# Moving score products ahead of the weighted sums in the first rounds of an attention and mixture kernel

## The chip, the cores and the metric

The kernel runs on one core of a Trainium2 chip. The metric is the time of one execution in microseconds (us), as the median of several runs. A profile of one execution shows, engine by engine, when each instruction ran. The engines are TensorE (PE, with its weight loads shown apart as PEld), VectorE (DVE), ScalarE (ACT), GpSimd (POOL, which here mostly issues transfers) and SyncE (SP).

## The reference

The inputs are q, k and v of shape (4 batches, 8 heads, 768 positions, 64), a flag per head, and the weights of 8 experts. First comes attention with one of two masks per head:

```python
scores = scale * np.matmul(q, k.transpose(0, 1, 3, 2))
causal = rel >= 0
stream_keep = causal & (is_sink | in_win)      # 4 sink positions, window 64
mask = np.where(retr[0, :, 0, 0, None, None], full_mask, stream_mask)
a = softmax(np.where(mask, scores, -1e9))
x = (a @ v) reshaped to (3072, 512)
```

Then the 3072 rows of x go through a mixture: the gate's exponentials P are normalised eight times by rows and columns (Sinkhorn), and the result is

```python
for e in range(8):
    h = np.maximum(x @ w1[e], 0.0)
    out += P[:, e:e + 1] * (h @ w2[e])
```

## The kernel before, in words

The work of attention is cut into units (b, g, u): a batch, a group of 256 query positions (g = 0, 1, 2) and a half of the heads. A unit has two halves a, each for two heads. Every half takes its keys in g + 1 chunks of up to 512 columns; such a chunk is a task, and two tasks make a round. For the first batch, counting from zero as the code does, round 0 is unit g=0,u=0; round 1 is g=0,u=1; rounds 2 and 3 are the halves a=0 and a=1 of g=1,u=0; rounds 4 and 5 are those of g=1,u=1; with round 6 the group g=2 begins. The names in the profile leave the batch out or the unit out: `PT_1_0_1` is g=1, u=0, a=1, and `sc_1_0` is a=1, chunk 0.

A round goes through these steps.

- `emit_prep` (L230): 16 transposes on PE turn the loaded k and q of a unit into the tile `tr`, and DVE copies it out as `kT` (L243).
- `scores(n)` (L479, with the products at L424): PE multiplies keys by queries into two tiles `sc` in PSUM. There are two such tiles and no more, so the products of a round wait until ACT has read those of the round before.
- `soften` (L482): with index 0 it issues the exponentials on ACT (L433, tile `PT`), with index 1 the masks on DVE (L442, L445).
- `sum_later(n)` and `finish_sums` (L472, L459): PE sums v by the masked weights (L268) into the one tile `pv`; DVE takes a reciprocal and scales (L281, L282) into `xn`. As there is one `pv`, the next sum waits for that scaling.
- `turn` (L289): four transposes of `xn` on PE, then an ACT copy (L299) into `xT`, which is x transposed, the input of the mixture.
- `fill` (L453): pieces of the first expert's layers, put between rounds so that PE has work. A piece of layer 1 (L334) reads `xT` and ends with a DVE relu (L341); a piece of layer 2 (L348) reads the weights w2 (`w_0_133`) and ends with an ACT copy (L352). The pieces of layer 1 read both `xT_76` (heads of u=0) and `xT_77` (heads of u=1).
- `place_v(g)` (L110): the v of the first batch is loaded with pairs of positions in one partition (`vraw`, the tile `acc_84`). Four products with an identity matrix (L115) put a third of it in order, and two ACT copies (L119) write it into the tile `v_0`.
- `emit_vfar` (L248): DVE multiplies v by the mask of far keys (`farx`) into `vf` (L252). The sums over far keys read `vf` instead of v. `spell_far(2, ...)` (L207) is an ACT copy that makes the third slice of `farx`, which the `vf` of group 2 needs.

The products of PE, the transposes, the pieces of the first expert and others share the tag `mo`, three banks of PSUM used in turn; a tile waits for the reader of the tile three before it.

The rounds 0 to 5 are written out by hand from L490 to L541, under `manual_schedule` for PE, DVE and ACT: on these engines the instructions stand in the order in which the code writes them. Loads of k, q and v are issued on POOL, where the framework places them; each waits for the eighth load before it. From round 6 on (L542) a loop writes the rounds, and the framework's scheduler may place their instructions among the others; it had, for instance, put the `vf` of group 2 in among the work of round 4. After attention come the Sinkhorn steps (L564) and the remaining seven experts (from L599), which take most of the time.

Of the kernel before, what the change touches and what calls it, by code (L numbers as in the profile page):

```python
# [32 lines left out]
def kernel(  # L33
# [61 lines left out]
    def v_tile(b):  # L95
        if b not in vts:
            vts[b] = ap.tile([128, H, NC, DV], F16, tag="v16", name=f"v16_{b}")
            nc.vector.memset(vts[b][:, :, :, D:DV], 1.0)
        return vts[b]
# [10 lines left out]
    def place_v(g):  # L110
        for n in range(2):
            t = psA.tile([128, 512], F32, tag="mo", bufs=3, name=f"vp_{g}_{n}")
            rows = slice(64 * n, 64 * n + 64)
            for c in range(2):
                nc.tensor.matmul(  # L115
                    out=t[64 * c:64 * c + 64, :].rearrange("p (h d) -> p h d", h=H),
                    lhsT=ident16[rows, rows], rhs=vraw[g][rows, :, c, :], start=True, stop=True,
                )
            nc.scalar.activation(  # L119
                out=v_tile(0)[:, :, 2 * g + n, 0:D], in_=t.rearrange("p (h d) -> p h d", h=H),  # L120
                func=AF.Copy, bias=0.0, scale=1.0,
            )
# [73 lines left out]
    farx = cp.tile([128, H, 3, DV], F16, tag="farx")  # L196
# [10 lines left out]
    def spell_far(n, src):  # L207
        nc.scalar.activation(out=farx[:, :, n], in_=src, func=AF.Copy, bias=0.0, scale=1.0)
# [21 lines left out]
    def emit_prep(b, g, u):  # L230
        tr = psA.tile([128, 512], F32, tag="mo", bufs=3, name=f"tr_{b}_{g}_{u}").bitcast(F16)
        for i, src in enumerate(kq[b, g]):
            for a in range(2):
                for c in range(2):
                    for hh in range(2):
                        nc.tensor.transpose(
                            out=tr[64 * hh:64 * hh + 64, ts(4 * i + 2 * a + c, 128)],
                            in_=src[:, 4 * u + 2 * a + hh, c, :], identity=ident16,
                        )
        t = ap.tile([128, 2, 2, 256], F16, tag=f"kT{u}{g}", bufs=1 + (g == 0),  # L240
                    name=f"kT_{b}_{g}_{u}")
        kTs[b, g, u], qTs[b, g, u] = t[:, 0], t[:, 1]
        nc.vector.tensor_copy(  # L243
            out=t.rearrange("r i a (n c p) -> r (i a) c n p", c=2, p=64),
            in_=tr.rearrange("r (i c n p) -> r i c n p", i=4, c=2, p=64),
        )

    def emit_vfar(b, g):  # L248
        if b not in vfs:
            vfs[b] = ap.tile([128, H, 4, DV], F16, tag="vf", bufs=1, name=f"vf_{b}")  # L250
        n = 2 * g - 2
        nc.vector.tensor_tensor(out=vfs[b][:, :, n:n + 2, :], in0=vts[b][:, :, n:n + 2, :],  # L252
                                in1=farx[:, :, g - 1:g + 1, :], op=ALU.mult)
# [35 lines left out]
    def turn():  # L289
        while turns:  # L290
            b, g, u = turns.pop(0)
            xn = xns.pop((b, g, u))
            xt = psA.tile([128, 512], F32, tag="mo", bufs=3, name=f"xt_{b}_{g}_{u}").bitcast(F16)
            for a in range(2):
                for sb in range(2):
                    nc.tensor.transpose(out=xt[:, ts(2 * a + sb, 128)], in_=xn[:, a, sb],
                                        identity=ident16)
            c0 = b * S + 256 * g
            nc.scalar.activation(  # L299
                out=xT[u][:, :, c0:c0 + 256], in_=xt[:, 0:512].rearrange("p (a c) -> p a c", a=2),  # L300
                func=AF.Copy, bias=0.0, scale=1.0)
            if u == 1:
                one, two = first_steps(b, g)
                at = len(fillers) - 2 * ((b, g) == (0, 1))
                fillers[at:at] = one
                fillers.extend(two)
# [18 lines left out]
    def first_steps(b, g):  # L325
        w1, w2 = expw[0]
        c0 = b * S + 256 * g
        hT = [hp.tile([128, 512], F16, tag="hT", name=f"hT_0_{b}_{g}_{i}") for i in range(4)]

        def layer1(i):  # L330
            l1 = psA.tile([128, 512], F32, tag="mo", bufs=3, name="l1")
            for fb in (2 * i, 2 * i + 1):
                for dc in range(4):
                    nc.tensor.matmul(  # L334
                        out=l1[:, ts(fb % 2, 256)], lhsT=w1[:, dc, ts(fb, 128)],
                        rhs=xT[dc // 2][:, dc % 2, c0:c0 + 256], start=(dc == 0), stop=(dc == 3),
                    )
            if late[0]:
                nc.scalar.activation(out=hT[i], in_=l1, func=AF.Relu, bias=0.0, scale=1.0)
            else:  # L340
                nc.vector.tensor_scalar(out=hT[i], in0=l1, scalar1=0.0, scalar2=None, op0=ALU.max)  # L341
            return 1

        def layer2(sb):
            l2 = psA.tile([128, DM], F32, tag="mo", bufs=3, name="l2")
            for fc in range(8):
                o = 256 * (fc % 2) + 128 * sb
                nc.tensor.matmul(  # L348
                    out=l2, lhsT=hT[fc // 2][:, o:o + 128], rhs=w2[:, fc, :],
                    start=(fc == 0), stop=(fc == 7),  # L350
                )
            nc.scalar.activation(out=acc_of(b * NC + 2 * g + sb),  # L352
                                 in_=l2.rearrange("p (n d) -> p n d", n=2), func=AF.Copy,
                                 bias=0.0, scale=1.0)
            return 2

        return [partial(layer1, i) for i in range(4)], [partial(layer2, sb) for sb in range(2)]
# [3 lines left out]
    def run(g, n):  # L361
        for _ in range(n):
            if next(g, "end") == "end":
                return False
        return True
# [29 lines left out]
    PTs, sums, preps = {}, [], []  # L395
# [57 lines left out]
    def fill(n):  # L453
        while n > 0 and fillers:
            done = fillers.pop(0)()
            n -= done
            left[0] -= done

    def finish_sums(between=None):  # L459
        for i, ((gen, scale), key) in enumerate([(sums_of[key], key) for key in sums_of]):  # L460
            if i and between:
                between()
            while run(gen, 1):
                pass
            del sums_of[key]
            scale[0]()
# [5 lines left out]
    def sum_later(n):  # L472
        for i, a, ci in tasks[2 * n:2 * n + 2]:
            b, g, u = units[i]
            if ci == g:
                scale = []
                sums_of[i, a] = gen_pv(b, g, u, a, PTs.pop((i, a)), scale), scale

    def scores(n):  # L479
        return [emit_scores(*t) for t in tasks[2 * n:2 * n + 2]]  # L480

    def soften(pairs, which=(0, 1)):  # L482
        for pair in pairs:
            for w in which:
                pair[w]()

    def warm(n):
        keep_warm(ident16, kTs[units[0]].rearrange("p a s -> p (a s)"), n)

    engines = {mybir.EngineType.PE, mybir.EngineType.DVE, mybir.EngineType.Activation}  # L490
    with tc.manual_schedule(engines=engines):
        keep_warm(blank[:, 0:128], blank, 9)
        make_far()
        make_keep()
        round_first(0)
        emit_prep(*units[0])
        round_first(4)
        r0 = scores(0)
        soften(r0, (0,))
        make_masks((0, 1))  # L500
        emit_prep(*preps.pop())
        warm(3)
        r1 = scores(1)
        soften(r1[:1], (0,))
        place_v(0)
        soften(r0, (1,))
        sum_later(0)
        soften(r1[1:], (0,))
        make_masks((2, 3))
        emit_prep(*preps.pop())  # L510
        warm(2)
        r2 = []
        finish_sums(lambda: r2.extend(scores(2)))
        soften(r1, (1,))
        soften(r2, (0,))
        warm(2)
        turn()
        sum_later(1)
        emit_vfar(0, 1)
        finish_sums(lambda: emit_prep(*preps.pop()))  # L520
        place_v(1)
        soften(r2, (1,))
        sum_later(2)
        r3 = scores(3)
        soften(r3, (0,))
        turn()
        spell_far(2, farx[:, :, 1])
        finish_sums()
        soften(r3, (1,))
        sum_later(3)  # L530
        fill(1)
        soften(scores(4))
        finish_sums()
        sum_later(4)
        fill(1)
        emit_prep(*preps.pop())
        soften(scores(5))
        turn()
        finish_sums()
        sum_later(5)  # L540
        fill(2)  # L541
    for n in range(6, rounds):  # L542
        soften(scores(n))
        if n == 7:
# [305 lines left out]
```

## Time and profile before

| what | value |
|---|---|
| median of 6 runs | 709.06 us (708.17 to 710.2) |
| the profiled execution, its own time | 709.68 us |
| its span from the first to the last instruction | 707.9 us |
| PE busy | 687.4 us, 97% of the span |
| DVE busy | 569.2 us, 80% |
| ACT busy | 418.0 us, 59% |
| POOL busy | 151.4 us, 21% |
| mean granted TensorE clock | 0.996 of full speed |
| the change's stretch: from the transposes of round 0 to the scores of round 6 | 17.05 to 30.88 us after the span's start |

The page of the profile gives shares over the whole span. The stretch that the change touches is 2% of it, so it has to be read from views of that stretch: the instructions in order of time, the waits, and the busy time in short windows. A start in the timeline is counted from the start of the span. Ends of matmuls are modelled, and an instruction's shown time holds its latency: the next one on the same engine often starts before the shown end. The clock column is what the throttle granted to TensorE, 1.00 being full speed.

### The profile page before, as it was taken

What the parts mean: (1) busy time and instruction counts of PE and PEld (TensorE: products, weight loads), DVE (VectorE), ACT (ScalarE), POOL (GpSimd) and SP (SyncE); (2) the same over time, 40 slices, a digit from 0 to 9 for tenths busy, and PEclk for the clock granted to TensorE, in tenths of its full rate; (3) what the DMA queues carried; (4) which work ended last, traced back from release to release, by engine and by line L of the source; (5) the groups of instructions that cost most, each with busy time, mean ns of one, the idle gap of its engine ahead of it and who ended that gap; (6) DMA issues with size and microseconds to landing.
All of it is one profiled execution on the core that took longest, in us unless ns stands there. A gap on an engine that the chain in (4) does not pass through costs nothing.

```text
span 707.9 us, 17061 instructions
## 1 busy us (share of the span) xinstructions
PE 687.4 (97%) x6932; PEld 569.8 (80%) x6932; DVE 569.2 (80%) x1157; ACT 418.0 (59%) x780; POOL 151.4 (21%) x183
## 2 busy tenths in 40 slices
PE   7899999999999999999999999999999999999995
PEld 3566666666588888888888888888888888888884
DVE  6657666756889988888898879887898889877886
ACT  6677777775795555555555555555555555555550
POOL 7422220000012122122212222122212221121210
PEclk9999999999999999999999999999999999999999
DMA  9999393000723378345933594349433954345774
GB/s 179 184 183 99 36 102 31 2 2 1 119 45 69 68 118 136 55 79 90 152 61 64 94 158 77 58 69 164 86 59 68 145 102 76 60 75 109 148 160 123
DMA packets 84223, 65.61 MB, mean 93 GB/s; under 512 B 48304, under 2 KB 64688, under 8 KB 84144
## 3 DMA queue, kind: packets, MB, share of 16 engines
q0 software_dynamic: 74976, 57.17, 56.9%
q1 hardware_dynamic: 7536, 6.30, 3.6%
q8 instruction: 54, 0.88, 0.5%
q10 hardware_dynamic: 1632, 1.05, 0.5%
q14 instruction: 25, 0.20, 0.1%
HBM read 52.45 MB, written 6.29 MB: 83 GB/s over the span
## 4 chain that ended last, share of the span: by engine, by line
PE 60%; DVE 1%; issue 0%; ACT 0%; DVEq 0%
PE l1y L670 17%; PE l2y L738 17%; PE l2w L738 9%; PE l1w L670 9%; PE l2z L738 4%; PE l1z L670 4%; DVE acc_84 L755 1%; DVE S_7_5_10640 L608 0%; DVE S_7_5_10643 L608 0%; DVE S_7_5_10642 L608 0%; DVE acc_83 L755 0%; ACT R_4602 L679 0%; DVEq L845 0%; DVE S_7_5_10641 L608 0%
## 5 line engine op out<-in xcount | busy, mean ns | idle before, releaser
L752 ACT ACTIVATE add<-l2w,Pne 128x256 f32<-128x256 f32 x80 | 33.6, 473 | 66.0 <-PE l2w L738 64.2
L334 PEld LDWEIGHTS <-w_0_126 128*128 128x128 f16 x384 | 35.9, 99 | 7.2 <-issue 3.1
L752 ACT ACTIVATE add<-l2y,Pne 128x256 f32<-128x256 f32 x80 | 33.7, 473 | 11.3 <-PE l2y L738 10.2
L752 ACT ACTIVATE add<-l2z,Pne 128x256 f32<-128x256 f32 x80 | 33.6, 472 | 8.7 <-PE l2z L738 8.7
L760 POOL DMA_DIRECT2D acc_79<-add x21 | 17.7, 844 | 78.8 <-ACT add L752 60.7
L760 POOL DMA_DIRECT2D acc_81<-add x21 | 17.7, 844 | 68.9 <-ACT add L752 67.1
L760 POOL DMA_DIRECT2D acc_80<-add x21 | 17.7, 845 | 67.9 <-ACT add L752 67.9
L760 POOL DMA_DIRECT2D acc_82<-add x21 | 17.8, 847 | 67.2 <-ACT add L752 67.2
L760 POOL DMA_DIRECT2D acc_83<-add x18 | 15.1, 840 | 54.4 <-ACT add L752 47.2
L760 POOL DMA_DIRECT2D acc_84<-add x18 | 15.4, 856 | 45.0 <-ACT add L752 38.3
L755 DVE SCALAR_TENSOR_TENSOR acc_79<-l2y,Pne,acc_79 128x256 f32<-128x256 f32 x42 | 18.3, 476 | 7.2 <-PE l2y L738 7.1
L755 DVE SCALAR_TENSOR_TENSOR acc_83<-l2y,Pne,acc_83 128x256 f32<-128x256 f32 x44 | 19.1, 476 | 3.2 <-PE l2y L738 3.2
L755 DVE SCALAR_TENSOR_TENSOR acc_82<-l2y,Pne,acc_82 128x256 f32<-128x256 f32 x42 | 18.2, 476 | 4.1 <-PE l2y L738 4.1
L755 DVE SCALAR_TENSOR_TENSOR acc_81<-l2y,Pne,acc_81 128x256 f32<-128x256 f32 x42 | 18.2, 476 | 4.1 <-PE l2y L738 4.1
L755 DVE SCALAR_TENSOR_TENSOR acc_80<-l2y,Pne,acc_80 128x256 f32<-128x256 f32 x42 | 18.2, 476 | 4.0 <-PE l2y L738 4.0
L755 DVE SCALAR_TENSOR_TENSOR acc_84<-l2y,Pne,acc_84 128x256 f32<-128x256 f32 x36 | 15.6, 476 | 7.1 <-PE l2y L738 7.1
L670 PEld LDWEIGHTS <-S_2_3734 128*128 128x128 f16 x192 | 18.8, 98 | 2.7 <-issue 0.5
L670 PEld LDWEIGHTS <-S_5_6872 128*128 128x128 f16 x192 | 18.8, 98 | 2.2
L670 PEld LDWEIGHTS <-S_3_4804 128*128 128x128 f16 x192 | 18.8, 98 | 2.2
L670 PEld LDWEIGHTS <-S_4_5838 128*128 128x128 f16 x192 | 18.8, 98 | 2.2
L670 PEld LDWEIGHTS <-S_6_7906 128*128 128x128 f16 x192 | 18.8, 98 | 2.2
L670 PEld LDWEIGHTS <-S_7_8940 128*128 128x128 f16 x192 | 18.8, 98 | 2.2
(2581 smaller groups left out, 2264.1 us busy)
## 6 DMA issues: line engine op xcount, KB each, us to landing
acc_79<-add POOLq DMA_DIRECT2D x21, 256.0 KB, 3.3
acc_80<-add POOLq DMA_DIRECT2D x21, 256.0 KB, 3.3
acc_81<-add POOLq DMA_DIRECT2D x21, 256.0 KB, 3.3
acc_82<-add POOLq DMA_DIRECT2D x21, 256.0 KB, 3.3
acc_83<-add POOLq DMA_DIRECT2D x18, 256.0 KB, 3.4
acc_84<-add POOLq DMA_DIRECT2D x18, 256.0 KB, 10.0
w_0_126<-in_moe_w_dram POOLq DMA_DIRECT2D x1, 1024.0 KB, 11.5
w_0_133<-in_moe_w_dram POOLq DMA_DIRECT2D x1, 1024.0 KB, 18.1
```

What stands on the lines that cost most here:

```text
L334: nc.tensor.matmul(out=l1[:, ts(fb % 2, 256)], lhsT=w1[:, dc, ts(fb, 128)], rhs=xT[dc // 2][:, dc % 2, c0:c0 + 256], start=(dc == 0), stop ...
L670: nc.tensor.matmul(out=banks[g, bank][:, f, :], lhsT=lefts1[e][k - 1][:, dc, ts(2 * g + f, 128)], rhs=rights1[c][k - 1][:, dc, :], start=( ...
L738: nc.tensor.matmul(out=banks[bank][q], lhsT=lefts2[e, c][k - 1][:, q, f, :], rhs=rights2[e][k - 1][:, f, :], start=(first and (final or q ...
L752: nc.scalar.activation(out=t[:, q, :], in_=banks[bank][q], func=AF.Copy, bias=0.0, scale=w)
L755: nc.vector.scalar_tensor_tensor(out=dst, in0=banks[bank][q], scalar=w, in1=dst, op0=ALU.mult, op1=ALU.add,)
L760: nc.gpsimd.dma_start(out=acc[c][:, i, n, :, :], in_=t, accum_op=ALU.add)
```

## The change

The change reorders the hand-written rounds 2 to 5. Nothing is computed that was not computed before, and nothing is left out.

- The products `scores(3)` move ahead of the sums of round 1, `scores(4)` ahead of the sums of round 2, and `scores(5)` ahead of the sums of round 4. Their exponentials (`soften(..., (0,))`) move with them, ahead of the masks of the preceding round where those are written later.
- `place_v(1)` moves ahead of the sums of round 1.
- `emit_vfar(0, 1)` moves behind the sums of round 1 and their scaling.
- `spell_far(2, ...)` moves from round 3 to behind the exponentials of round 5.
- The exponentials and the masks of rounds 4 and 5 are written apart. The prep of group 2 comes between the turn and the exponentials of round 5.
- The four pieces of `fill` are spread as 1, 1, 1, 1 instead of 1, 1, 2.

```diff
         sum_later(1)
+        r3 = scores(3)
+        place_v(1)
+        finish_sums(lambda: emit_prep(*preps.pop()))
+        soften(r3, (0,))
         emit_vfar(0, 1)
-        finish_sums(lambda: emit_prep(*preps.pop()))
-        place_v(1)
         soften(r2, (1,))
         sum_later(2)
-        r3 = scores(3)
-        soften(r3, (0,))
         turn()
-        spell_far(2, farx[:, :, 1])
+        r4 = scores(4)
         finish_sums()
         soften(r3, (1,))
+        soften(r4, (0,))
+        fill(1)
         sum_later(3)
+        finish_sums()
+        soften(r4, (1,))
         fill(1)
-        soften(scores(4))
+        r5 = scores(5)
+        turn()
+        emit_prep(*preps.pop())
+        soften(r5, (0,))
+        spell_far(2, farx[:, :, 1])
+        sum_later(4)
         finish_sums()
-        sum_later(4)
         fill(1)
-        emit_prep(*preps.pop())
-        soften(scores(5))
-        turn()
-        finish_sums()
+        soften(r5, (1,))
         sum_later(5)
-        fill(2)
+        fill(1)
     for n in range(6, rounds):
```

In the program as built, PE's instructions stand in the same order as before from the scores of round 6 on, and so do those of ACT. On DVE the `vf` of group 2 now stands after the relu of the fourth piece, ahead of the copy of the prep in round 6. On POOL the third of the four loads of the next batch's v goes ahead of the loads of k and q for its group 1.

## The prediction

> **What bounds the kernel now.** I read the page first, then what PE waited for over the whole span, then short windows of the stretch, then its timeline.
>
> ```profile
> span 707.9 us, 17061 instructions
> PE 687.4 (97%) x6932; PEld 569.8 (80%) x6932; DVE 569.2 (80%) x1157; ACT 418.0 (59%) x780; POOL 151.4 (21%) x183
> ...
> PE l_446 L334 <- ACT xT_77 L299: 1.6, 1, 1.6
> ...
> PE pv_0_1_1_381 L268 <- DVE xn_0_1_358 L282: 0.7, 1, 0.7
> ```
>
> The first two lines are the page's, the others come from PE's waits. PE is busy for 97% of the span and no later wait of PE is on a load, so PE's order sets the end: what PE gains before round 6 moves everything behind it. In the stretch of the change one wait stands out, a piece of the first expert (`l_446`) that waits 1.6 us for `xT_77`. The next view is busy time by window, with the granted clock as the third number from the end.
>
> ```profile
> core 0: us, PE busy (x) PEld busy (x) DVE busy (x) ACT busy (x) POOL busy (x), PEclk, DMA share, GB/s
> 16.56:19.98 3.42, 2.33 (x41) 1.46 (x41) 3.34 (x9) 1.44 (x4) 0.95 (x1) 1.00 1.57 187
> 19.98:23.39 3.41, 1.77 (x31) 1.26 (x28) 2.31 (x7) 3.41 (x6) 1.62 (x2) 1.00 1.61 192
> 23.39:26.80 3.41, 3.41 (x33) 2.21 (x31) 1.79 (x4) 1.94 (x3) 1.10 (x2) 0.50 1.27 208
> 26.80:30.21 3.41, 3.41 (x58) 2.79 (x57) 2.59 (x7) 1.89 (x3) 1.24 (x2) 1.00 1.92 180
> ```
>
> I laid the windows so that one of them is the stretch of low clock, which lasts from 23.4 to 26.8. It follows the window in which PE was busy for 1.77 of 3.41 us; the one with 2.33 of 3.42 us was not followed by one. This is the only low stretch that the records show in the span. ACT is busy for all of 19.98 to 23.39, and in the window before for 1.44 of 3.42 us: the late `xT_77` comes from ACT's order. The timeline says how.
>
> ```profile
> 19.16 0.36 PE L268 MATMUL pv_0_1_1_381<-v_0_256,PT_0_1_1_246 128*128 128x65 f16 x6 [0.72 <-DVE xn_0_1_358 L282]
> ...
> 19.79 0.39 PE L424 MATMUL sc_1_0_402<-kT_1_0_287,kT_0_0_189 64*128 64x256 f16 x4
> ...
> 19.89 0.60 ACT L119 ACTIVATE v_0_256<-vp_0_391 128x512 f16<-128x512 f32 x1 [1.91 <-PE vp_1_395 L115]
> 20.38 0.59 ACT L119 ACTIVATE v_0_256<-vp_1_395 128x512 f16<-128x512 f32 x1
> 20.86 1.03 ACT L433 ACTIVATE PT_1_0_1_401<-sc_1_0_402 128x1024 f16<-128x1024 f32 x1
> 21.76 0.83 ACT L433 ACTIVATE PT_1_0_1_401<-sc_1_1_407 128x768 f16<-128x768 f32 x1
> ...
> 22.45 0.63 ACT L299 ACTIVATE xT_77<-xt_0_1_414 128x512 f16<-128x512 f16 x1
> ...
> 23.14 0.38 PE L334 MATMUL l_446<-xT_77,w_0_126 128*128 128x256 f16 x2 [1.59 <-ACT xT_77 L299]
> ...
> 28.97 1.90 POOL L126 DMA_DIRECT2D v_1_308<-in_v_dram  x2 [3.63 <-DMA w_0_133<-in_moe_w_dram]
> ...
> 30.88 0.39 PE L424 MATMUL sc_0_0_585<-kT_2_0_516,kT_0_0_189 64*128 64x256 f16 x4
> ```
>
> ACT sat idle for 1.91 us, then had two v copies and two exponentials to do ahead of `xT_77`. PE meanwhile had time for the products that feed them: it was idle for 0.72 us at 18.4.
>
> **The change part by part**, each time against the profiled execution (span 707.9, time 709.68, which is 0.62 above the median).
>
> *Round 3's scores and v's second third, sooner.* PE is free at about 17.3 and both `sc` tiles are read by then (exponential of `sc_0_1`: 16.51 + 0.81 = 17.32). The eight products take 0.5 (19.79 to 20.28), the four of `place_v` 0.35 (19.44 to 19.79), so they end near 18.15. v's raw third is there: POOL's issue at 14.18 was already behind it. The sum of `pv_0_1_0` follows, then the prep, which now uses the bank of `xt_0_0`, free when its copy ends at 17.98. PE reaches the second sum of round 1 at 19.2, as before (19.16), because DVE's scaling decides that. So 0.85 us of PE work has moved into idle time, at no cost. On ACT the v copies run from 18.2 to 19.3 (spacing 0.49, length 0.60), the exponentials of round 3 from 19.2 to 20.9 (spacing 0.91, length 0.82), and `xT_77` from 20.85, right behind its transposes, to 21.45. Before it ended at 23.08: 1.6 us sooner.
>
> *The `vf` of group 1, later.* Before, it lay at 17.85 in time that DVE had free. Now it stands behind the scaling of `xn_0_1` (ends 20.3) and ahead of the masks of round 2: 0.70 long, 0.62 to the next. The masks end at 21.6 instead of 20.9. That puts about 0.6 us on PE, which does `scores(4)` meanwhile (0.46; its second tile waits until 20.95 for the exponential), so some 0.35 shows.
>
> *Rounds 2 to 5 from there.* The sum `pv_1_0_0` runs from 21.25 to 21.85; the first piece (`l_446` before) needs `xT_77` (21.45) and runs 0.87 without a wait (29.04 to 29.91 shows that length) to 22.7. The sum of round 3 needs DVE's scaling (22.05 + 0.2 + 0.42) and masks (0.20 + 0.55, to 23.35): PE waits 0.24 and 0.22 and ends at 23.6. From here PE finds everything ready: a piece to 24.5, `scores(5)` to 24.95, transposes 25.2, the prep (0.5) 25.7, the sum of `pv_1_1_0` 26.15, two pieces (1.74) 27.9. The exponentials of round 5 wait on ACT behind the copy of `xT_76`, until 25.9, and end at 27.6; ahead of round 6 they are hidden by the two pieces. So the scores of round 6 start at 27.9 to 28.1 instead of 30.88: 2.9 us sooner. PE's work in between is 8.4 us at full clock, counted by starts. Before, 13.8 us passed: 8.4 of work, 1.5 from the low clock, 3.9 of waits. After, 10.9: waits 2.5, low clock 0. The sum is −1.4 (waits) −1.5 (clock) = −2.9.
>
> *The far copy and group 2's `vf`, later.* The copy (0.68 on ACT) comes just ahead of round 6's exponential and delays it by at most 0.2; the `vf` (0.70 on DVE) was in an idle place (DVE waited 0.46 ahead of it) and now delays the copy of the prep for g=2,u=1, whose `kT` is first read at 39.49. DVE then waits for ACT (1.77 before), so both are covered; without the cover they would cost 0.2 and 0.7.
>
> *POOL and the loads.* The third v load moves from 28.97 to about 22.7; k and q of the next batch's group 1 move back one place each, q from 24.45 to 28.97. With 13.1 us to landing, q is there at 43 and first read at 52.83, some 50 now: nothing. But w2 (`w_0_133`) is first read at 32.42 before and at about 29.5 now, and it landed near 28.97, when POOL's wait for it ended. The margin shrinks from 3.4 to 0.5 us. The v load that now runs beside it is 192 KB, 1.0 us at 187 GB/s, in place of 256 KB of q: between nothing and 0.5 us on PE. I take nothing, as the bytes beside it are fewer.
>
> *The clock, the one large unknown.* The row says that a window with a half idle PE costs the next one half its clock, without any gap longer than 1.59 us. The Trainium skill speaks differently: "TensorE: Matmul & The Clock Gate", section "Why this matters for your kernels", holds PE warm as long as no idle gap exceeds about 3 us. By it the change takes away no cause of the low stretch, and only the 1.4 us of waits would go: 708.3. By the row the drop goes too if PE's busy share in each window stays above some value between 1.77 and 2.33 of 3.41. In the same place (19.98 to 23.39) I count about 2.5 after the change; in the worst place (18.9 to 22.3) 2.2. The same page, Part 1, calls the window free-running; only one execution is at hand here to say that. So where the windows fall may differ by execution, before and after. I go by the row: no low stretch in most executions. Bounds: 0 to −1.5.
>
> Nothing later is timed by a clock of its own: waits of the Sinkhorn steps and of the experts are on other engines and move along. 709.68 − 2.9 = 706.8. I do not take it from the median as well, since the profiled execution shows the low stretch that goes, and faster ones (708.17) may be without it.
>
> **The rivals.**
>
> *The clock drop stays or moves* (for it: 2.2 lies under 2.33; the sum of small waits, 0.3, 0.95, 0.16 and 0.15, lies in one window; against: 2.2 is nearer to 2.33 than to 1.77). Then only the waits go: 708.3, up to 708.6 if the low window falls on the densest work.
>
> *w2 comes late, or other handoffs eat a part* (for it: a margin of 0.5 us; against: fewer bytes beside it). One us later costs 0.5, two cost 1.5: 707.3 to 708.3, I say 707.6.
>
> *Slower: low windows in a row.* If PE's waits, now spread, leave several windows below the threshold between 17 and 34 us, each costs 1.5. One gives 708.3, two 709.8, three 711.3. It decides from the third on. Against it: a low window fills itself (3.41 of 3.41 busy before, and the clock came back after one).
>
> *The order does not do what is said*: no sign, since the built program has the new order on PE, ACT and DVE.
>
> **How the numbers follow.** The forecast (706.8, its own range 705.9 to 707.5) has 0.58, the staying drop 0.22, the late w2 0.13, low windows in a row 0.06, and 0.01 is left. 0.2% of 709.06 is 1.4 us, about what a measurement of this kernel can tell from no change: faster means below 707.64, slower above 710.48. Faster gets the forecast almost whole (0.57), half of the late w2 (0.07) and a quarter of the staying drop (0.06): 0.70. Slower gets the row of low windows less its milder part: 0.05. The rest, 0.25, is the same. The range runs from the forecast's low end 705.9 to 708.5, which takes in most of the staying drop.
>
> **What would show it.** Right: `xT_77` copied near 21, no wait of PE above 0.9 us between 17 and 28, the first piece without a wait on ACT, a clock of 1.00 in all windows, the scores of round 6 near 28.0, and the same lead of 2.9 us at the first layer-2 piece. Wrong: a window at 0.50 anywhere between 17 and 34; a wait of the first L348 on `w_0_133`; a lead that shrinks between round 6 and the end of the span.

## The result and the profile after

The changed kernel takes 707.18 us (median of 10 runs, 706.31 to 709.37), the kernel before in the same comparison 709.0 (20 runs, 707.5 to 711.68): a ratio of 0.9972, 95% interval 0.9961 to 0.9983. The profiled execution took 707.37. A second comparison, made with the last experiments, gave 707.86 against 709.51, ratio 0.9976 (0.9966 to 0.9986).

The page and PE's waits over the whole span, after:

```profile
span 705.6 us, 17059 instructions
PE 686.3 (97%) x6932; PEld 569.1 (81%) x6932; DVE 568.7 (81%) x1157; ACT 417.7 (59%) x780; POOL 151.3 (21%) x183
...
PE l_1029 L334 <- ACT xT_77 L299: 0.8, 1, 0.8
...
PE xt_0_1_414 L296 <- DVE xn_0_1_375 L282: 0.7, 1, 0.7
```

The wait of the first piece for `xT_77` is gone from the list. The 0.8 that is left with that name belongs to a later piece (at 54.8 us before, at 52.4 after) and stood in the kernel before too. The 0.7 for DVE's scaling has changed its place: the second sum used to wait for it, now the transposes behind that sum do.

The windows, laid again by the record of the clock, whose steps fall at 14.93 and every 3.41 us from there:

```profile
14.93:18.34 3.41, 2.97 (x40) 1.66 (x38) 2.66 (x8) 2.83 (x4) 0.17 (x1) 1.00 1.23 202
18.34:21.76 3.42, 2.55 (x52) 1.69 (x48) 2.92 (x8) 3.28 (x6) 1.51 (x2) 1.00 1.82 182
21.76:25.17 3.41, 3.24 (x48) 2.46 (x46) 2.89 (x10) 1.54 (x2) 1.96 (x3) 1.00 1.32 207
25.17:28.58 3.41, 3.41 (x58) 2.68 (x56) 2.91 (x8) 2.74 (x4) 0.27 (x1) 1.00 1.64 194
```

PE is busy for 2.55 us in the emptiest of them, and the clock stays at 1.00 throughout. These windows lie elsewhere against the work than those of the kernel before, so one has to ask whether their place alone spared the change. Moved over the stretch by tenths of a us, a window of 3.41 us is never emptier after the change than here:

```profile
17.20:20.61 3.41, 2.44 (x44) 1.54 (x44) 2.78 (x9) 3.12 (x6) 0.95 (x1) 1.00 1.70 183
```

In the kernel before, every window that begins between 19.6 and 21.6 holds less than 1.9 us of PE's work. That is 2.0 of 3.41 us of possible places, so I estimate from this one execution that about six executions in ten of the kernel before had such a window. The timeline shows why PE is busier now:

```profile
17.33 0.29 PE L296 MATMUL xt_0_0_343<-ident_93,xn_0_0_300 128*128 128x128 f16 x2 [0.19 <-DVE xn_0_0_300 L282]
17.55 0.39 PE L424 MATMUL sc_1_0_350<-kT_1_0_287,kT_0_0_189 64*128 64x256 f16 x4
...
18.48 0.60 ACT L119 ACTIVATE v_0_256<-vp_0_360 128x512 f16<-128x512 f32 x1 [0.23 <-PE vp_1_364 L115]
...
20.64 0.28 PE L296 MATMUL xt_0_1_414<-ident_93,xn_0_1_375 128*128 128x128 f16 x2 [0.70 <-DVE xn_0_1_375 L282]
...
21.05 0.63 ACT L299 ACTIVATE xT_77<-xt_0_1_414 128x512 f16<-128x512 f16 x1
...
22.34 0.38 PE L334 MATMUL l_458<-xT_77,w_0_126 128*128 128x256 f16 x2
...
28.52 0.39 PE L424 MATMUL sc_0_0_585<-kT_2_0_532,kT_0_0_189 64*128 64x256 f16 x4
...
30.07 0.59 PE L348 MATMUL l_635<-w_0_133,hT_0_0_0_420 128*128 128x512 f16 x2
```

ACT's idle time ahead of the v copies has shrunk from 1.91 to 0.23 us, `xT_77` is copied at 21.05 instead of 22.45, and the piece that begins at 22.12 on `xT_76` goes on to `xT_77` at 22.34 without a wait.

I measure what follows as the **stretch**: from the second pair of transposes of round 0 to the scores of round 6. It was 13.83 us (17.05 to 30.88) and is 11.19 us (17.33 to 28.52): 2.64 less. This execution reached the stretch 0.28 later, which leaves a lead of 2.36 at round 6. At the first layer-2 piece it is 2.35 (32.42 before, 30.07 after), at the first Sinkhorn product 2.3 (161.8 before, 159.5 after), and at the end of the span it is 2.3 (707.9 and 705.6). Nothing is given back on the way.

### The profile page after: what moved, and what is told of

Same layout as the page of the kernel before. It is cut to its first block, busy times and chain, and to the rows that moved or that the text cites. A ratio compares the mean times of both kernels' runs of the same rounds, so it can differ in the third digit from the quotient of the medians.

```text
span 705.6 us, 17059 instructions
## 1 busy us (share of the span) xinstructions
PE 686.3 (97%) x6932; PEld 569.1 (81%) x6932; DVE 568.7 (81%) x1157; ACT 417.7 (59%) x780; POOL 151.3 (21%) x183
## 4 chain that ended last, share of the span: by engine, by line
PE 60%; DVE 1%; issue 0%; ACT 0%; DVEq 0%
PE l1y L675 17%; PE l2y L743 17%; PE l2w L743 9%; PE l1w L675 9%; PE l2z L743 4%; PE l1z L675 4%; DVE acc_84 L760 1%; DVE S_7_5_10640 L613 0%; DVE S_7_5_10643 L613 0%; DVE S_7_5_10642 L613 0%; DVE acc_83 L760 0%; ACT R_4602 L684 0%; DVEq L850 0%; DVE S_7_5_10641 L613 0%
```

## The experiments

The forecast gave two parts, 1.4 us of waits and 1.5 us of clock. The rule that speaks against the second part was the rival to test first. Single profiles give the stretch; runs against the kernel before on the same chip give the ratio, with an interval of about ±0.001, which is 0.7 us. Differences of a few tenths of a us can be read only in the stretch, and of each kernel in the table one execution was profiled; of the change there is a second one, whose stretch was 11.18 us. In the traces of the experiments the tile names stand without numbers.

| kernel | ratio (95% interval) | stretch us | `xT_77` copied, us from the stretch's start |
|---|---|---|---|
| before | 1 | 13.83 | 5.40 |
| the change | 0.9972 (0.9961 to 0.9983) | 11.19 | 3.72 |
| part one alone | 0.9970 (0.9960 to 0.9981) | 11.61 | 3.71 |
| the other part alone | 1.0002 (0.9993 to 1.0011) | 14.83 | 5.39 |
| before with a busy gap | 0.9986 (0.9977 to 0.9994) | 12.63 | 5.40 |
| far product early again | 0.9969 (0.9958 to 0.9981) | 11.01 | 3.71 |
| v's third alone | 0.9981 (0.9971 to 0.9991) | 11.63 | 4.44 |
| round 3's scores alone | 0.9970 (0.9958 to 0.9981) | 11.00 | 3.81 |
| round 3's scores, changed late rounds | 0.9972 (0.9961 to 0.9983) | 10.79 | 3.80 |

### The clock by itself: a busy gap

```diff
         sum_later(3)
+        busy = psA.tile([128, 512], F32, tag="mo", bufs=3, name="keep_on")
+        for _ in range(6):
+            nc.tensor.matmul(out=busy, lhsT=ident16, rhs=..., start=True, stop=True)
         fill(1)
```

> The kernel before, with six products of 512 columns (1.3 us, their result is read by nobody) put into PE's 1.6 us wait for xT_77; no order is changed and no other instruction moves. Theory (a window of some 3.4 us with PE half idle costs the next one half its clock): no window at 0.50 between 20 and 34, the wait for xT_77 shrinks to 0.4 but its end stays at 23.1, and the time falls only by the clock's part: 0.6 to 1.3 us in the median, ratio 0.9982 to 0.9992. Rival (the clock falls only after a gap above 3 us, and the low stretch has another cause): the stretch of low clock is there as before, ratio 1.000.

The time fell by a ratio of 0.9986, 708.14 against 709.31 us. PE's timeline of this kernel, then its windows by the record of the clock:

```profile
21.64 1.46 PE L533 MATMUL keep_on<-kT,ident 128*128 128x512 f16 x6
22.94 0.38 PE L334 MATMUL l<-xT,w 128*128 128x256 f16 x2
23.61 0.82 PE L334 MATMUL l<-xT,w 128*128 128x256 f16 x6 [0.30 <-ACT xT L299]
...
17.65:21.07 3.42, 2.52 (x49) 1.69 (x48) 3.35 (x10) 1.44 (x4) 0.95 (x1) 1.00 1.78 182
21.07:24.48 3.41, 3.06 (x32) 1.78 (x31) 2.06 (x6) 3.02 (x5) 1.83 (x2) 1.00 1.43 201
24.48:27.89 3.41, 3.29 (x60) 2.39 (x57) 2.54 (x7) 2.35 (x3) 0.89 (x1) 1.00 1.50 196
```

`xT_77` is as late as before (5.40 us into the stretch), yet there is no low window and the stretch is 12.63: products that nobody reads save 1.20 us. Nor did the place of the windows spare this execution: the one that holds 3.06 us here (21.07 to 24.48) would hold 1.77 in the kernel before, at the same distance from the stretch's start (20.59 to 24.00). The 1.20 us are the clock's part. What the change saves beyond it, 12.63 − 11.19 = 1.44, is by subtraction the part of the waits. The rival, that no gap under 3 us can cost the clock, has fallen.

### Which half of the change

Part one is the edit around `scores(3)`, `place_v(1)` and the far product; the other part is everything from `r4 = scores(4)` on.

```diff
 part one alone                                   the other part alone
+        r3 = scores(3)                           (rounds 1 to 3 as before)
+        place_v(1)                                       turn()
         finish_sums(lambda: emit_prep(...))     +        r4 = scores(4)
+        soften(r3, (0,))                                 finish_sums()
+        emit_vfar(0, 1)                                  soften(r3, (1,))
         soften(r2, (1,))                        +        soften(r4, (0,))
         ... (rounds 4 and 5 as before)                   ... (as changed)
```

> Part one of the change alone: scores of round 3 and v's second third ahead of the sums of round 1, the far product of group 1 behind them; rounds 4 and 5 written as before. Theory (late copy of xT_77 and the low clock it causes): xT_77 is copied near 21 as with the whole change, the 1.6 us wait of the first piece goes, and with it the low window; the scores of round 6 start some 2.3 us sooner than before (waits -1.1, clock where it was low -1.2), so 707.0 to 707.6, ratio 0.9970 to 0.9985. Rival (the gain comes from the later rounds' scores ahead of their sums): less than 0.5 us, ratio 0.9993 or above.

> The other part alone: rounds 1 to 3 up to the turn as before, then the scores of rounds 4 and 5 ahead and the far copy later. Theory: the first piece still waits about 1 us or more for xT_77, the clock still drops in most executions, gain at most 0.3 us, ratio 0.9995 to 1.000. Rival (the later rounds carry the gain): 1.5 us or more, ratio 0.998 or below.

Part one alone gives 0.9970 and a stretch of 11.61, with no low window in it. The other part alone gives 1.0002. Its waits and windows:

```profile
PE sc L424 <- ACT PT L433: 1.3, 1, 1.3
...
18.51:21.92 3.41, 1.89 (x36) 1.19 (x31) 2.78 (x8) 1.59 (x3) 1.73 (x2) 1.00 1.80 178
21.92:25.34 3.42, 2.86 (x28) 1.91 (x28) 0.79 (x4) 3.23 (x5) 1.94 (x3) 0.51 1.30 207
25.34:28.74 3.40, 3.40 (x28) 2.41 (x28) 2.49 (x8) 0.00 (x0) 0.00 (x0) 0.50 1.65 188
28.74:32.15 3.41, 3.41 (x58) 2.81 (x54) 2.44 (x5) 2.56 (x4) 2.84 (x4) 0.99 2.18 171
```

The scores of round 4 now stand where the first piece stood, and wait 1.3 us for the exponentials, since ACT is as late as before: one wait in place of another. The clock fell to half again, and this time for two windows. So the gain comes from part one. The other part, put behind it, shortens the stretch by another 11.61 − 11.19 = 0.42 us, which the ratios cannot show.

### Which edit of part one

In the first kernel only `place_v(1)` moves ahead of the sums of round 1; in the second only `scores(3)` with its exponentials does. In both, the far product stays where it was.

```diff
 v's third alone                       round 3's scores alone
+        place_v(1)                    +        r3 = scores(3)
         emit_vfar(0, 1)               +        soften(r3, (0,))
         finish_sums(...)                       emit_vfar(0, 1)
-        place_v(1)                             finish_sums(...)
                                                place_v(1)
                                       ...
                                       -        r3 = scores(3)
                                       -        soften(r3, (0,))
```

> The kernel before with v's second third alone moved ahead of the sums of round 1; the scores of round 3 stay behind them. Theory (the gain is the filling of ACT's 1.9 us of idle time ahead of the v copies, whatever fills it): the v copies run there, the copy of xT_77 starts near 21.3 instead of 22.45, PE's wait for it falls from 1.6 to about 0.5 us, and with that the window is busy enough to keep the clock: stretch from the transposes of round 0 to the scores of round 6 near 12.0 us (before 13.8), ratio 0.9976 to 0.9985. Rival (the scores' being ahead is what counts): ratio 0.9990 or above.

> The kernel before with the scores of round 3 and their exponentials alone moved ahead of the sums of round 1; v's second third stays behind them, and the far product of group 1 stays early. Theory (filling ACT's idle time is what counts): the exponentials run from 17.9 to 19.6, the v copies behind them, xT_77 is copied near 20.7 to 21.0, the wait goes and the clock stays: stretch of 11.2 to 11.7 us, ratio 0.9970 to 0.9978, as much as the whole change. Rival (both moves are needed): half of the gain, ratio 0.9985 or above.

ACT's timeline, first with v's third alone, then with the scores alone:

```profile
17.82 1.08 ACT L119 ACTIVATE v<-vp 128x512 f16<-128x512 f32 x2
19.84 1.73 ACT L433 ACTIVATE PT<-sc 128x1024 f16<-128x1024 f32 x2 [0.93 <-PE sc L424]
21.45 0.60 ACT L299 ACTIVATE xT<-xt 128x512 f16<-128x512 f16 x1
```

```profile
17.36 1.72 ACT L433 ACTIVATE PT<-sc 128x1024 f16<-128x1024 f32 x2
19.39 1.08 ACT L119 ACTIVATE v<-vp 128x512 f16<-128x512 f32 x2 [0.30 <-PE vp L115]
20.36 0.60 ACT L299 ACTIVATE xT<-xt 128x512 f16<-128x512 f16 x1
```

Either edit fills ACT's idle time, and neither leaves a low window. The scores alone, 1.6 us of ACT work, fill it nearly whole; the v copies, 1.0 us, leave 0.93 of it. The scores alone reach a stretch of 11.00, as short as the whole change, and 0.9970. v's third sooner is not needed once the scores are ahead. With v's third alone the stretch (11.63) is as long as that of part one, but the ratio is 0.9981, and PE still waits 0.60 us for `xT_77`; the intervals of the two ratios overlap, so which of these is its worth stays open.

### The far product, and the scores alone with the late rounds

```diff
 far product early again                 round 3's scores, changed late rounds
+        emit_vfar(0, 1)                          r3 = scores(3)
         r3 = scores(3)                  +        soften(r3, (0,))
         place_v(1)                      +        emit_vfar(0, 1)
         finish_sums(...)                         finish_sums(...)
         soften(r3, (0,))                +        place_v(1)
-        emit_vfar(0, 1)                 -        (all three where the change has them)
```

> The changed kernel with one edit taken back: the far product of group 1 stands again ahead of the sums of round 1, in time that DVE has free. Theory: the masks of round 2 end 0.6 us sooner and PE's waits behind them shrink by 0.2 to 0.3: ratio to the kernel before 0.0003 below that of the change (0.9972), about 0.9969. Rival (DVE's place there is covered by the scores of round 4): the same as the change, 0.9972.

> The changed kernel with v's second third put back behind the sums of round 1, the exponentials of round 3 and the far product of group 1 ahead of them: the scores alone of round 3 moved, with the changed rounds 4 and 5. Theory: 0.3 to 0.4 us less than the whole change, since the far product leaves the chain of DVE and the v copies leave the way of the exponentials: stretch of 10.8 us (11.2 with the change), ratio 0.9963 to 0.9970. Rival (DVE's scaling of the sums sets this part whatever ACT does): the same as the change, 0.9972.

The far product early gives a stretch of 11.01, 0.18 less than the change, and 0.9969: below what the ratio can tell, so the rival is not refuted by the time. The scores alone with the late rounds have the shortest stretch of all (10.79, as expected), but a ratio of 0.9972. In that profile the stretch began at 18.35, a full us later than in the change's. The gain of 0.4 is therefore seen in the stretch alone, and the expected ratio (0.9970 or less) was missed.

### The same cause at another place: the start

Looking for low windows in the change's record I found a stretch that the prediction had not spoken of, two windows from 8.11 to 14.93 us. The views of the kernel before show 1.00 there, but its eight transposes at 9.89 take 0.64 us, and eight of the same shape at 13.41 take 0.41: the record of that trace has its first entry only at 13.16. Ahead of the low stretch PE waits 2.3 us for the first rounded k, and in it 0.8 us for the first `kT`.

```diff
-        keep_warm(blank[:, 0:128], blank, 9)
+        keep_warm(blank[:, 0:128], blank, 14)
         ...
         round_first(4)
+        keep_warm(blank[:, 0:128], blank, 2)
         r0 = scores(0)
```

> The changed kernel with seven more products that nobody reads ahead of the first scores: five more on the nine at the start, two behind the first transposes, where PE waits for loads and for DVE. Theory (a window of 3.4 us with PE under about 2 us busy costs the next one half its clock, here too): the stretch of 0.50 between 8 and 15 us shrinks or goes, transposes take 0.41 instead of 0.64 there, and the sums of round 0 start 0.4 to 0.7 us sooner: ratio 0.9962 to 0.9967. Rival (that stretch waits for loads, not for PE): the same as the change, 0.9972, or worse by the 0.1 to 0.2 us that the products may delay the first transposes.

The ratio is 0.9960 (0.9945 to 0.9976), 706.06 us. PE's timeline and waits:

```profile
8.08 0.60 PE L258 MATMUL warm<-xT 128*128 128x512 f16 x2
...
9.37 0.41 PE L236 MATMUL tr<-ident,k 128*64 128x128 f16 x8
...
15.94 0.28 PE L296 MATMUL xt<-ident,xn 128*128 128x128 f16 x2 [0.19 <-DVE xn L282]
...
27.12 0.61 PE L424 MATMUL sc<-kT,kT 64*128 64x256 f16 x8
...
28.99 1.90 PE L348 MATMUL l<-w,hT 128*128 128x512 f16 x8 [0.16 <-DMA w<-in_moe_w_dram]
```

The transposes take 0.41, the stretch starts at 15.94 instead of 17.33 and lasts 11.18 as with the change. That is 1.39 us sooner, twice the expected. It is not an accident of one execution: the ten that were profiled with the start as before, whatever their later order, began the stretch between 16.55 and 18.35, the three with the busy start (this one and two below) between 15.93 and 16.33. Of the 1.39 us 1.08 is left at the first piece of layer 2, partly because PE now waits 0.16 us for w2: the margin of 0.5 us of which the prediction spoke is used up.

Next I moved the load of w2 one place forward, and then also took the scores alone instead of the whole part one. The change itself ran beside them.

```diff
-        vraw.append(load_v_pairs(2))
         expw[0] = (expw[0][0], load_w2(0))
+        vraw.append(load_v_pairs(2))
```

> The changed kernel with the seven products more at the start, and with the load of w2 issued one place earlier, ahead of v's last third. Theory (with the busy start PE reaches the first piece of layer 2 before w2 has landed, and waits for it until 28.99): w2 lands 1 to 1.5 us sooner, the wait goes, the first L348 starts near 28.6, and the products of v's last third, read near 31, find their load landed: 0.2 to 0.4 us less than the busy start alone, ratio 0.9955 to 0.9960. Rival (the next thing is late at once: v's last third): no gain over 0.9960.

> As the kernel before in this list, and with v's second third back behind the sums of round 1 (exponentials of round 3 and the far product of group 1 ahead of them). Theory: the stretch is 0.4 us shorter (10.8 against 11.2, as the scores alone with the changed late rounds showed), so 0.3 to 0.4 us less again, ratio 0.9950 to 0.9957. Rival (that 0.4 was lost again, since the scores alone with the late rounds measured the same ratio as the change): no gain over the run without it.

> The changed kernel itself, for a comparison on one chip with the runs beside it. Theory: 0.9972 as on record, within 0.0008; the runs beside it lie 0.0012 and 0.0017 below. Rival (the differences between the versions were differences between chips and calls): all three within 0.0005.

On one chip, against 709.51 for the kernel before: the change 707.86, ratio 0.9976 (0.9966 to 0.9986); with the busy start and w2 sooner 705.95, 0.9952 (0.9939 to 0.9965); with all three 705.49, 0.9946 (0.9931 to 0.9960). Both stand clear of the change and of the kernel before, by twice what was expected (0.0024 and 0.0030 below the change, where 0.0012 and 0.0017 were forecast). In neither does the first L348 wait for w2. The step between these two, 0.0006, is within the intervals; in the profiles the stretch goes from 11.31 (16.33 to 27.64) to 10.79 (15.93 to 26.72). The gain of w2 alone cannot be told either: the run without it was made in another comparison, and the expected start of L348 near 28.6 was missed (29.19), in part because this execution waited 0.29 us more for a `kT` at 14.69.

## Why the prediction was right

**The size.** 706.8 was forecast, within 705.9 to 708.5; the median is 707.18, the profiled execution 707.37. Against the sum, the stretch was to last 10.9 us and took 11.19; the rest is the start, which came 0.28 later in this execution. No part of the change did that, but the clock: at 12.21 this execution was 0.07 ahead, and then the low stretch of the start lasted to 14.93 instead of 13.16, so that the transposes at 13.54 took 0.64 us where those at 13.41 took 0.41.

The closeness of the median owes something to the starting point. The medians differ by 1.8 us (1.65 in the second comparison), not by 2.9 or by the 2.64 of the stretch. The forecast took its 2.9 from a profiled execution that was 0.62 slower than the median; taken from the median, it would have been 706.2. The reason given for that choice, that faster executions may be without the low stretch, fits the estimate of six in ten, but no run shows it, so this part of the closeness has to pass for luck.

**The waits, −1.4.** By subtraction −1.44. The step behind it held to the tenth: scores and v's third went into PE's idle time and pulled `xT_77` forward by 1.68 us within the stretch (1.6 forecast). What it credited too widely is the part of v: the scores alone do the same.

**The clock, −1.5.** Measured −1.20 by the busy gap. I had taken nearly the whole half of 3.41 us. At full clock part of that is lost in waits again: in the kernel with the busy gap, the transposes of g=1,u=0 (27.32) take 0.69 us where they took 0.40 before, since they wait 0.29 for DVE's scaling. The choice between the trace's row and the page's rule was the right one: the rule of the Trainium skill ("TensorE: Matmul & The Clock Gate", section "Why this matters for your kernels"), no gap above about 3 us, would have left the low window in place, and here it came with no gap longer than 1.59 us. The 2.2 us of PE's work that I feared in the worst place are 2.44 by the trace, more than the 2.33 that kept the clock in the kernel before.

**The far product, +0.35.** Measured +0.18, by putting it back, from one profile of that kernel. It lies in DVE's chain; that the scores of round 4 cover more of it than I took would explain the difference, but is not shown.

**Loads and w2.** No cost was forecast and none was seen after the change: the first L348 started at 30.07 without a wait. That the margin was short showed with the busy start, where the wait came.

**The rivals.** The staying drop did not come in the profiled executions of the change (11.19 and, again, from 17.53 to 28.71, 11.18). Low windows in a row are real, but where the order leaves PE idle: they came in the kernel with the other part alone. My argument against them, that a low window fills itself, was wrong: with 2.86 of 3.42 us busy at half clock, the next window was low again.

**What was overlooked.** I wrote that the stretch from 23.4 to 26.8 was the only low one that the records show. But for the last 1.8 us of the span, where PE has no work left, that is so, but the durations at the start told of another, and the largest gain found beyond the change lay there. The expectation of 1.00 in all windows was missed for that reason too: it came true from 14.93 to the end of PE's work.

## What to carry to other kernels

Before moving work into an idle place, find which engine's idle time makes the wait: here PE waited, but ACT's 1.9 us of idle ahead of the wait were what had to be filled, and the scores alone, which fill them nearly whole, brought as much as the whole change. Then ask of each window of some 3.4 us how long PE is busy in it, since here each window that was about half idle cost the next one half its clock; where nothing useful can be moved in, products that nobody reads can be worth their place. And when the record of the clock shows nothing, compare the durations of equal instructions.

## What the runs showed of the hardware

- The clock fell after windows with PE busy for 1.77 (before) and 1.89 (the other part alone) of 3.41 us, and stayed after windows with 2.33 (before), 2.52 (the busy gap), 2.55 (the change), 2.59 (v's third alone) or more. Where the edge lies between 1.89 and 2.33 was not tried.
- Once low, it stayed low after a window with 2.86 us busy (the other part alone), and came back after windows with 3.29 (v's third alone, 9.09 to 12.50), 3.40 and 3.41. In these runs it took more to get the clock back than to keep it.
- The record of the clock can be silent on a low stretch near the start: the views show 1.00 at 9.89 in the kernel before, with transposes of 0.64 us where 0.41 is the length at full clock. For that reason the mean granted clock of the span does not compare the two kernels: it is 0.996 before and 0.994 after, since only the trace after has the low stretch of the start on record.
- The low stretch costs the median and not single executions alone: the busy gap moved the median by 1.2 us (709.31 to 708.14; by the ratio 0.4 to 1.6), about as much as the profiled stretch.
